# Second products of a feed-forward block, run as two 64-row halves on the TensorE array

## The chip, the cores and the metric

One NeuronCore of a Trainium2 chip runs the whole kernel. The metric is the device time of one execution in microseconds, from launch to the last store. All inputs and the output lie in the chip's memory as fp32.

## The reference, cut to what matters

An input of 2048 positions by 576 channels is normalised over the channels. Two branches read the result, and their sum is added to the input: a state-space convolution along the positions (computed in the kernel as a transform, a product with a kernel spectrum and a transform back), and a feed-forward block of width 4608.

```python
x = A_u
xn = _layernorm(x, axis=-1)
return x + _A_ref(xn, A_A_re, ..., A_Dskip) + _B_ref(xn, B_w1, B_w2)

def _B_ref(x, w1, w2):
    h = jnp.einsum("bsd,df->bsf", x, w1)     # 576 -> 4608, the first product
    h = _silu(h)
    out = jnp.einsum("bsf,fd->bsd", h, w2)   # 4608 -> 576, the second product
    return out
```

## The kernel before, in words

The positions are worked in two halves of 1024, each of two blocks of 512, and the width of 4608 in nine chunks (`NCH`) of four tiles (`FT`) of 128. For every (half, chunk, block) the function `up` computes the first products of the four tiles, and `down` the second products of the block's four groups of 128 positions.

Both products are done in fp32r, a one-pass form of fp32 with a shortened mantissa. To keep precision each operand is split into a high part and a low part, and three products are added: high by high, high by low and low by high. So a first product (`ph`, L331 to L333) is 14 matmuls that move 512 columns each into one PSUM bank. A second product (`po`, L357) covers half of the 576 output channels: 12 matmuls (four tiles of the width, three part products each) that move 288 columns and contract over 128 rows, all adding up in one bank. VectorE then adds that bank to the running sum `acc[j]` in SBUF (L361). There are 288 such sums, so 3,456 second-product matmuls and 288 adds.

The eight PSUM banks are shared by three pools: `ps1` with two banks (the first products), `ps2` with three (the second products, and now and then another tile), and `pss` with three (transposes and everything of the convolution branch).

Beside the feed-forward block runs the convolution branch, as a generator `side()` that is woven into it step by step. Between about 165 and 640 us it builds the convolution kernel: VectorE and ScalarE make tables (`th`, `S`, `C`), TensorE contracts them (`kp`, L696, on columns 32 wide) and transforms the result (`z`, L711). Those `z` matmuls already work on 64-row halves of the array: the two halves of `kt` go to the two halves of the array by `tile_position=(64 * h, 0)`, in turns, each into a bank of its own. From about 640 us on it multiplies the spectra (`pk`, `pu2`, `pb`, L826). In the tail it adds the convolution's result to the running sums (`py`, L847, tiles of 64 rows by 32 columns).

The order of instructions on each engine is not the order of the source. A scheduler decides it at build time: it runs its own model of the engines, picks among the instructions that are ready, and takes the adds of `down` ahead of other VectorE work (`tc.high_priority()`). A tile is given a bank when one is free in that model. Once built, each engine runs its list in order and waits at semaphores.

Of the kernel before, what the change touches and what calls it, by code (L numbers as in the profile page):

```python
# [11 lines left out]
F32 = mybir.dt.float32  # L12
# [7 lines left out]
P = 128  # L20
# [6 lines left out]
HD = D // 2  # L27
# [16 lines left out]
def kernel(  # L44
# [21 lines left out]
    nc = tc.nc  # L66
    FT = 4
# [40 lines left out]
    ps1 = ctx.enter_context(tc.tile_pool(name="ps1", bufs=2, space=PSUM))  # L108
    ps2 = ctx.enter_context(tc.tile_pool(name="ps2", bufs=3, space=PSUM))
    pss = ctx.enter_context(tc.tile_pool(name="pss", bufs=3, space=PSUM))  # L110

    acc = {}
# [27 lines left out]
    pins = {}  # L140
# [27 lines left out]
    def load_x(j, pool, tag, engines):  # L168

        t = pool.tile([P, 2, D], F32, tag=tag, name=f"{tag}{j}")  # L170
        for i in range(2 if j == 0 else 1):
            for ps, v, eng in quarters(xv, engines):
                if j:
                    eng.dma_start(t[ps], v[:, j:j + 2])
                else:
                    eng.dma_start(t[ps, i], v[:, i])
        pairs[j] = t
        return t[:, 0, :], t[:, 1, :]
# [78 lines left out]
    def ffn():  # L257
        w2v = w2.rearrange("(t p) d -> p t d", p=P)
        blocks = [(half, c, b) for half in range(2) for c in range(NCH) for b in range(2)]
        W1, W2, G = {}, {}, {}  # L260
# [83 lines left out]
        def down(blk, jj):  # L344
            half, c, b = blk
            j = 8 * half + 4 * b + jj
            js = slice(jj * P, (jj + 1) * P)
            if half == 1 and c == NCH - 1:
                if jj % 2 == 0:
                    add_conv(j, (acc[j], acc[j + 1]))  # L350
            for h in range(2):
                hs = slice(h * HD, (h + 1) * HD)
                po = ps2.tile([P, 512], F32, tag="ps2", name="po")
                n = 0
                for t in range(FT):
                    for g, w in ((0, 0), (0, 1), (1, 0)):
                        pins["pe"] = nc.tensor.matmul(po[:, :HD], G[blk, t][g][:, js], W2[half, c, t][w][:, hs],  # L357
                                                      start=n == 0, stop=n == 3 * FT - 1).ins
                        n += 1
                with tc.high_priority():  # L360
                    nc.vector.tensor_add(acc[j][:, hs], po[:, :HD], acc[j][:, hs])  # L361
            if half == 0 and c == NCH - 1:
                rows = slice(j * P, (j + 1) * P)
                nc.sync.dma_start(dr0[rows, :], acc[j])
                if j % 2:
                    acc[7 + j], acc[8 + j] = load_x(7 + j, accp, "acc", (nc.sync,))
# [42 lines left out]
        for i, blk in enumerate(blocks):  # L409
            half, c, b = blk  # L410
# [23 lines left out]
            for step in ("u0", "d0", "d1", "d2", "d3", "u1", "u2", "u3"):  # L434
                k = int(step[1])
                if step[0] == "d":
                    down(blk, k)
                    yield 3.0
                elif later:
                    up(blocks[i + 1], k)  # L440
                    yield 3.0
                for f, t in after.get((b, step), ()) if more else ():
                    f(*new, t)
                if half == 0 and c == NCH - 1:
                    for kt in {"d3": (0, 1), "u1": (2, 3), "u2": (4,)}.get(step, ()):
                        split_xt(b, kt)
# [391 lines left out]
    def add_conv(j, dsts):  # L838

        py = [pool.tile([P, 512], F32, tag=t, name="py") for pool, t in ((pss, "pss"),) * 3 + ((ps2, "ps2"),)]  # L840
        first = pins["pe"]
        for n in range(16):
            i, q1, q2, h = 1 - n // 8, n // 4 % 2, n // 2 % 2, 1 - n % 2
            o = 64 * q1 + 32 * q2
            rows = slice(64 * h, 64 * h + 64)
            with tc.high_priority() if n else nullcontext(), behind(first):
                mm = nc.tensor.matmul(py[2 * i + h][o:o + 32, :HD], s4[rows], yss[j + i][rows, 2 * q2 + q1],  # L847
                                      start=True, stop=True, tile_position=(64 * h, o), skip_group_check=True)
            if n == 0:
                first = mm.ins  # L850
        for i in range(2):
            del yss[j + i]
            for h in range(2):
                hs = slice(h * HD, (h + 1) * HD)
                nc.vector.tensor_add(dsts[i][:, hs], py[2 * i + h][:, :HD], dsts[i][:, hs])
        for _ in range(2):
            conv_load()
# [165 lines left out]
```

## Time and profile before

| | |
|---|---|
| median of the runs before | 1111.05 us (1110.82 to 1111.27, two runs) |
| span of the profiled execution | 1108.2 us |
| profiled execution's own time | one of these two runs; some 2.6 to 3.1 us lie outside its span |
| TensorE matmul busy | 1102.2 us, 99% |
| VectorE busy | 916.6 us, 83% |
| ScalarE busy | 706.9 us, 64% |
| GpSimd busy | 72.1 us, 7% |
| chain that ended last | TensorE 98%: second products (L357) 42%, first products (L331 to L333) 41% |
| moved by DMA | 148.56 MB, 134 GB/s on the mean |

The profile shows one execution. PE is TensorE's matmuls, PEld its weight loads, DVE is VectorE, ACT ScalarE, POOL GpSimd and SP the queue that issues most transfers. Matmuls overlap in the array's pipeline, so the duration of one is longer than the distance to the next; what a matmul costs is that distance. "128*128" beside a matmul is the part of the array it uses, rows by columns; "x16" is a count. A row of the timeline has the start, the length, the engine and the instruction.

### The profile page before, as it was taken

What the parts mean: (1) busy time and instruction counts of PE and PEld (TensorE: products, weight loads), DVE (VectorE), ACT (ScalarE), POOL (GpSimd) and SP (SyncE); (2) the same over time, 40 slices, a digit from 0 to 9 for tenths busy, and PEclk for the clock granted to TensorE, in tenths of its full rate; (3) what the DMA queues carried; (4) which work ended last, traced back from release to release, by engine and by line L of the source; (5) the groups of instructions that cost most, each with busy time, mean ns of one, the idle gap of its engine ahead of it and who ended that gap; (6) DMA issues with size and microseconds to landing.
All of it is one profiled execution on the core that took longest, in us unless ns stands there. A gap on an engine that the chain in (4) does not pass through costs nothing.

```text
span 1108.2 us, 22917 instructions
## 1 busy us (share of the span) xinstructions
PE 1102.2 (99%) x9167; PEld 997.5 (90%) x9167; DVE 916.6 (83%) x1543; ACT 706.9 (64%) x1222; POOL 72.1 (7%) x129
## 2 busy tenths in 40 slices
PE   9999999999999999999999999999999999999998
PEld 7989998899998899899999989999999999999887
DVE  7799899999999999999999737787778778784433
ACT  4564466676677676677867536877777878774210
POOL 1100000000000000011000000000000000000111
PEclk9999999999999999999999999999999999999999
DMA  9745512525252525264744173554544455434983
GB/s 270 190 123 160 152 50 61 120 73 131 77 121 83 116 72 118 77 174 154 206 122 103 45 179 109 162 167 123 156 145 152 138 149 170 129 107 127 241 224 87
DMA packets 175755, 148.56 MB, mean 134 GB/s; under 512 B 111088, under 2 KB 142592, under 8 KB 175520
## 3 DMA queue, kind: packets, MB, share of 16 engines
q1 hardware_dynamic: 165328, 112.63, 38.7%
q0 software_dynamic: 9568, 33.62, 9.6%
q8 instruction: 72, 1.18, 0.5%
q10 hardware_dynamic: 752, 0.85, 0.3%
q14 instruction: 35, 0.29, 0.1%
HBM read 102.53 MB, written 44.61 MB: 133 GB/s over the span
## 4 chain that ended last, share of the span: by engine, by line
PE 98%; DMA 1%; DVE 1%; SPq 0%; issue 0%; DVEq 0%
PE po L357 42%; PE ph L331 35%; PE kp L696 3%; PE ph L332 3%; PE ph L333 3%; PE pu L826 2%; PE pb L826 2%; PE pk L826 2%; PE z L711 2%; PE pu L161 1%; PE py L847 1%; DMA acc<-in_A_u_dram 1%; PE pu L162 1%; PE pt L124 0%; DVE w1l L295 0%; PE ptk L490 0%
## 5 line engine op out<-in xcount | busy, mean ns | idle before, releaser
L357 PE MATMUL po<-w2l,gh 128*128 128x288 f32 x1152 | 338.5, 295 | 0.0
L357 PE MATMUL po<-w2h,gl 128*128 128x288 f32 x1152 | 336.4, 295 | 0.0
L357 PE MATMUL po<-w2h,gh 128*128 128x288 f32 x1152 | 336.1, 295 | 0.0
L357 PEld LDWEIGHTS po<-w2h,gh 128*128 128x128 f32 x1152 | 215.2, 188 | 7.7 <-issue 2.8
L357 PEld LDWEIGHTS po<-w2l,gh 128*128 128x128 f32 x1152 | 215.9, 188 | 5.1 <-issue 0.5
L357 PEld LDWEIGHTS po<-w2h,gl 128*128 128x128 f32 x1152 | 215.4, 188 | 0.9
L339 ACT ACTIVATE gf<-ph 128x512 f32<-128x512 f32 (+1 forms) x148 | 86.4, 584 | 143.8 <-PE ph L333 134.8
L331 PE MATMUL ph<-xh,w1l 128*128 128x512 f32 (+1 forms) x592 | 161.3, 385 | 0.0
L331 PE MATMUL ph<-xh,w1h 128*128 128x512 f32 (+1 forms) x592 | 161.3, 387 | 0.0
L331 PE MATMUL ph<-xl,w1h 128*128 128x512 f32 (+1 forms) x592 | 161.1, 385 | 0.0
L361 DVE TENSOR_TENSOR acc<-po,acc 128x288 f32<-128x288 f32 x288 | 126.2, 451 | 37.0 <-PE po L357 35.6
L342 DVE TENSOR_TENSOR gl<-gf,gh 128x512 fp32r<-128x512 f32 (+1 forms) x148 | 99.0, 672 | 64.6 <-ACT gh L340 63.8
L331 PEld LDWEIGHTS ph<-xh,w1l 128*128 128x128 f32 x592 | 108.0, 188 | 20.0
L331 PEld LDWEIGHTS ph<-xl,w1h 128*128 128x128 f32 x592 | 107.9, 188 | 19.8
L331 PEld LDWEIGHTS ph<-xh,w1h 128*128 128x128 f32 x592 | 104.5, 188 | 16.7 <-ACT x L133 0.5
L340 ACT CAST gh<-gf 128x512 fp32r<-128x512 f32 (+1 forms) x148 | 89.5, 608 | 9.5 <-PE po L357 6.6
L653 ACT ACTIVATE c<-th,magic 128x1040 f32<-128x1040 f32 x36 | 42.1, 1168 | 37.9 <-DVE C L676 28.0
L655 ACT ACTIVATE c<-th 128x1040 f32<-128x1040 f32 x36 | 38.7, 1075 | 33.6 <-DVE th L654 33.6
L314 ACT CAST w2h<-w2r 128x576 fp32r<-128x576 f32 x72 | 47.0, 671 | 17.7 <-PE po L357 14.9
L295 DVE TENSOR_TENSOR w1l<-w1r,w1h 128x640 fp32r<-128x640 f32 x72 | 56.9, 817 | 0.2
L332 PE MATMUL ph<-x,w1h 128*128 128x512 f32 (+1 forms) x148 | 57.0, 386 | 0.0
L333 PE MATMUL ph<-x,w1l 128*128 128x512 f32 (+1 forms) x148 | 56.9, 385 | 0.0
(185 smaller groups left out, 1828.8 us busy)
## 6 DMA issues: line engine op xcount, KB each, us to landing
w2r<-in_B_w_dram SPq DMA_DIRECT2D x72, 288.0 KB, 3.8
w1r<-in_B_w_dram SPq DMA_DIRECT2D x35, 512.0 KB, 3.8
d1u<-u POOLq DMA_DIRECT2D x32, 288.0 KB, 2.5
d1k<-stage SPq DMA_DIRECT2D x18, 512.0 KB, 6.8
ur<-d1u SPq DMA_DIRECT2D x32, 288.0 KB, 3.7
kr<-d1k SPq DMA_DIRECT2D x32, 288.0 KB, 2.9
d<-yo POOLq DMA_DIRECT2D x32, 288.0 KB, 4.0
ys<-d SPq DMA_DIRECT2D x32, 288.0 KB, 11.8
```

What stands on the lines that cost most here:

```text
L295: pins["w1l"] = nc.vector.tensor_sub(l1, src, h1).ins
L314: pins["w2h"] = nc.scalar.copy(h2, r2).ins
L331: nc.tensor.matmul(ph, w[:, kt, :], v[:, kt, a:e], start=n + kt == 0, stop=False)
L332: nc.tensor.matmul(ph, h1[:, 4, :], x4[:, a:e], start=False, stop=False)
L333: pins["pe"] = nc.tensor.matmul(ph, l1[:, 4, :], x4[:, a:e], start=False, stop=True).ins
L339: nc.scalar.activation(gf, ph, AF.Silu)
L340: pins["gh"] = nc.scalar.copy(gh, gf).ins
L342: pins["gl"] = nc.vector.tensor_sub(gl, gf, gh).ins
L357: pins["pe"] = nc.tensor.matmul(po[:, :HD], G[blk, t][g][:, js], W2[half, c, t][w][:, hs], start=n == 0, stop=n == 3 * FT - 1).ins
L361: nc.vector.tensor_add(acc[j][:, hs], po[:, :HD], acc[j][:, hs])
L653: nc.scalar.activation(c65, th, AF.Identity, bias=magic)
L826: nc.tensor.matmul(dst, st, mv[:, hs], start=n == 0, stop=n == 3 * len(terms) - 1)
```

## The change

Each matmul of a second product becomes two, over rows 0 to 63 and 64 to 127 of the same operands, at array positions (0, 0) and (64, 0). Each half of the contraction adds up in a bank of its own, so a sum of 12 matmuls in one bank becomes 24 in two banks. The banks come from `ps2`, except that the second bank of every fourth sum comes from `ps1`. VectorE adds both banks to the running sum, one after the other, 576 adds in place of 288.

```diff
             for h in range(2):
                 hs = slice(h * HD, (h + 1) * HD)
-                po = ps2.tile([P, 512], F32, tag="ps2", name="po")
+                po = [pool.tile([P, 512], F32, tag=t, name="po")
+                      for pool, t in ((ps2, "ps2"), (ps1, "ps1") if h and jj % 2 else (ps2, "ps2"))]
                 n = 0
                 for t in range(FT):
                     for g, w in ((0, 0), (0, 1), (1, 0)):
-                        pins["pe"] = nc.tensor.matmul(po[:, :HD], G[blk, t][g][:, js], W2[half, c, t][w][:, hs],
-                                                      start=n == 0, stop=n == 3 * FT - 1).ins
+                        for r in range(2):
+                            rows = slice(64 * r, 64 * r + 64)
+                            pins["pe"] = nc.tensor.matmul(po[r][:, :HD], G[blk, t][g][rows, js],
+                                                          W2[half, c, t][w][rows, hs], start=n == 0,
+                                                          stop=n == 3 * FT - 1, tile_position=(64 * r, 0)).ins
                         n += 1
                 with tc.high_priority():
-                    nc.vector.tensor_add(acc[j][:, hs], po[:, :HD], acc[j][:, hs])
+                    for r in range(2):
+                        nc.vector.tensor_add(acc[j][:, hs], po[r][:, :HD], acc[j][:, hs])
```

## The prediction

> **What bounds the kernel now.** I read the page first: its busy shares, the chain that ended last and the costliest groups.
>
> ```profile
> span 1108.2 us, 22917 instructions
> ...
> PE 1102.2 (99%) x9167; PEld 997.5 (90%) x9167; DVE 916.6 (83%) x1543; ACT 706.9 (64%) x1222; POOL 72.1 (7%) x129
> ...
> PEclk9999999999999999999999999999999999999999
> ...
> PE 98%; DMA 1%; DVE 1%; SPq 0%; issue 0%; DVEq 0%
> ...
> L357 PE MATMUL po<-w2l,gh 128*128 128x288 f32 x1152 | 338.5, 295 | 0.0
> L357 PE MATMUL po<-w2h,gl 128*128 128x288 f32 x1152 | 336.4, 295 | 0.0
> L357 PE MATMUL po<-w2h,gh 128*128 128x288 f32 x1152 | 336.1, 295 | 0.0
> ```
>
> TensorE is the chain: 98% of the span, at full granted clock, never idle before a second product. The mean of 295 ns is the latency of one matmul, since they overlap; what one costs is the pace of a long run. The chain in order of time gives that:
>
> ```profile
> 625.59 6.36 PE po L357 x48
> 1061.51 6.55 PE po L357 x48
> ```
>
> 6.36 / 48 and 6.55 / 48 are 0.1325 and 0.1365 us. I take 0.133 us per second product, so 3,456 of them hold the array for 459.6 us, which agrees with the 42% the page gives L357 (465 us). Then I asked what TensorE waits for, and how full VectorE is in each stage (columns: stretch, length, then busy time of PE, PEld, DVE, ACT, POOL, granted clock, DMA share, GB/s).
>
> ```profile
> PE pz L879 <- DVE zero L874: 1.3, 1, 1.3
> PE pt L124 <- DVE xn L202: 0.4, 2, 0.2
> ...
> 165.00:640.00 475.00, 475.00 (x5083) 428.69 (x5082) 454.00 (x681) 327.98 (x495) 21.52 (x39) 1.00 0.40 108
> 640.00:915.00 275.00, 275.00 (x1728) 254.53 (x1727) 205.68 (x373) 199.80 (x413) 19.77 (x36) 1.00 0.51 150
> ```
>
> TensorE waits 1.7 us in all. VectorE is second: in the long stage it works 454 of 475 us, without ever holding TensorE up. So whatever TensorE is given or spared shows in the span nearly one for one.
>
> **The change part by part.** Each second product becomes two matmuls, over contraction rows 0 to 63 and 64 to 127. They still move 288 columns each. The kernel already has this shape of work: the z matmuls (L711) are 64-row halves of the array that take turns. Their rows price everything, in stretches of the timeline around 501 us (start, length, engine).
>
> ```profile
> 500.61 0.29 PE L357 MATMUL po<-w2l,gh 128*128 128x288 f32 x1
> 500.83 0.38 PE L711 MATMUL z<-f,kt 64*128 64x128 f32 x2
> 500.83 0.97 PEld L711 LDWEIGHTS z<-f,kt 64*128 64x128 f32 x16 [0.16 <-ACT gf L339]
> 500.94 0.41 PEld L711 LDWEIGHTS z<-f,kt 64*128 64x128 f32 x5
> 500.83 1.16 PE L711 MATMUL z<-f,kt 64*128 64x128 f32 x16
> 501.92 0.40 PE L161 MATMUL pu<-sp,s 128*128 128x288 f32 x1
> 502.16 0.29 PE L162 MATMUL pu<-sp,s 128*128 128x288 f32 x1
> 36.14 0.60 PE L124 MATMUL pt<-ident,xn 128*128 128x128 f32 x4
> ...
> L711 PEld LDWEIGHTS z<-f,kt x288: 182/188/189, 174.5 to 642.9; 64*128 64x128 f32 x144
> L711 PE MATMUL z<-f,kt x288: 272/272/374, 174.5 to 643.0; 64*128 64x128 f32 x144
> ```
>
> Four things follow. (1) Two halves do run side by side: the first two z matmuls span 0.38 us together, where one alone lasts at most 0.374, so the second starts under 0.01 us after the first. (2) A half is no cheaper than a whole: 16 z loads span 0.97 us with 0.188 each, so a pair comes every (0.97 - 0.188) / 7 = 0.112 us; four whole transposes (L124) of the same 128 columns come every (0.60 - 0.27) / 3 = 0.11 us. (3) The next load of a half is hidden behind its running matmul: loads go on from 500.94 while the first pair runs. (4) Changing between whole array and halves empties the array: from the last po at 500.61 to the second pu at 502.16 are 1.55 us, holding one po (0.133), 8 z pairs (0.892) and one pu (0.133), in sum 1.158. The other 0.39 us is the two changes, 0.195 us each, part of it the unhidden first load (0.40 against 0.29 for the pu).
>
> By (1) and (2) the best the change can reach for a pair is 0.133 us, what the whole matmul cost. It spares TensorE nothing; the question is what it adds.
>
> *The order.* The source issues the halves in turns, but a scheduler decides TensorE's order, and each half needs its own free bank. In the built program of the changed kernel the turns are often lost:
>
> ```
> L360 po_2824<-w2h_1873,gh_2196 [waits DVE] ... 12 matmuls of po_2824
> L161, L162 pu x4, L331 ph x4
> L360 po_2825<-w2h_1873,gh_2196 [waits DVE] ... 12 matmuls of po_2825
> ```
>
> po_2824 is the lower half, po_2825 the upper half of one sum. TensorE starts its matmuls in order, so twelve of one half in a row use half the array at a time, 0.133 us each. Of 6,912 half matmuls 4,255 follow one of the same half, 2,370 one of the other half, 287 something else. In 106 of the 288 sums the first half is through before the second begins. I walked the order with one rule (a matmul starts when its half is free and the matmul ahead has started): 1,353 start beside a partner, 5,559 take a slot of their own. 5,559 x 0.133 = 739 us against 459.6: **+280 us**. The pace is bounded by its nearest rows: 0.1365 above, and below by the 512-column products, 12 in 2.75 us, or 0.229 each (0.447 ns a column, 0.129 for 288):
>
> ```profile
> 1003.17 2.75 PE ph L331 x12
> ```
>
> *Array changes.* The scheduler weaves second products between first products (L331) and the spectral ones, all on the whole array. Changes of array shape in TensorE's order go from 88 to 561, that is 473 more x 0.195 = **+92 us**. Bounds: 0, if the emptying belongs to z's plain fp32 data and not to the shape, and 0.195 again for doubt above. Against 0: the transposes at 36.14 are plain fp32 on the whole array too, come between po matmuls, and pass at their ordinary pace.
>
> *VectorE.* 288 more adds of one 128x288 bank into the running sum:
>
> ```profile
> L361 DVE TENSOR_TENSOR acc<-po,acc 128x288 f32<-128x288 f32 x288 | 126.2, 451 | 37.0 <-PE po L357 35.6
> ...
> 165.00:640.00 475.00, 55.98 (x129) 1.00 0.40 108
> ```
>
> The second row is the long stage with this line alone. 288 x 0.451 = 130 us, 1,047 us in all. Over a span of some 1,480 us that is 71%, so it hides behind TensorE. In the long stage 129 of the adds fall, 454 + 58 = 512 us, where TensorE's 475 grows by a third or so. What isn't hidden is the wait for banks: a sum holds two banks of five shared with ph, and matmuls of the second product that wait for VectorE go from 301 to 572. Behind such a wait stands all of TensorE, also the first products, then the SiLU and casts on ScalarE. Bounds: 0, as now; and one add for each of the 288 sums, 130 us. I take **+40 us**, nearer to 0, because the order already fills most bank waits by running one half alone (priced above), and VectorE gets freer. At the very end one more add is exposed, **+0.4 us**.
>
> DMA queues: no transfer is added. Loads and stores keep their order within small swaps, and SP, POOL and ACT get more time per transfer as TensorE slows; the cover is TensorE's own work. Without it, nothing is late that isn't late now.
>
> *Sum.* 1108.2 + 280 + 92 + 40 + 0.4 = 1520.6 for the span; 2.9 more lie around it (1111.05 median less 1108.2). **1523 us**, against 1111.05.
>
> **The rivals.**
>
> - *No overlap.* Halves in fp32r on 64 rows aren't shown by any row. If none overlapped, 1,353 more slots of 0.133 are +180: 1703 us. Against it: the z rows. Chance 0.08.
> - *Order doesn't matter.* If each half of the array drained its own queue, the second products would stay at 460 us: 1523 - 280 = 1243. Against: in every row matmuls start in order. Chance 0.05.
> - *Free change of shape.* 1523 - 92 = 1431. For it: only fp32 matmuls are tiled now. Chance 0.06.
> - *Loads show.* If a load couldn't run behind a matmul of its own half, 5,559 slots grow by the unhidden load, 0.40 - 0.29 = 0.11 us: +611, about 2095 with the bank waits gone. Against: the z loads from 500.94, and a pair in 0.112. Chance 0.04. The Trainium skill (TensorE: Matmul & The Clock Gate, Part 3, The mechanism) states just this: a load overlaps running matmuls only where its row group differs. This trace disagrees, for whole-array and 64-row loads alike.
> - *VectorE holds the banks.* Each sum waits for one more add: 1523 + 90 = 1613. For it: 454 of 475 us. Against: TensorE slows more than VectorE is loaded. Chance 0.12.
> - *Not slower.* If a 64-row matmul in fp32r streamed in half the time, 0.0665, slots would fill 370 us, 90 less than now, and the shape changes would eat just that: 1108.2 - 90 + 92 + 3.3 = 1114. It decides from a half's price of 0.07 downward. Against: 0.112 for 64 rows beside 0.11 for 128. Chance 0.02.
>
> **How the numbers follow.** My forecast has 0.63. Its own range, from the pace (0.129 to 0.1365: -22 to +19) and the bank waits (-40 to +40), is some 1460 to 1585. The 8-in-10 range takes in the free change below and VectorE's wait above: 1430 to 1615; left out are 0.08 + 0.05 + 0.04 + 0.02. A measurement can tell about 2% here (22 us). Faster by that 0.01 and the same 0.01 share the last rival; slower has 0.98.
>
> **What would show it.** Right: TensorE still over 95% busy and on the chain; long runs of one half at 0.133 us a matmul; pairs starting within 0.01 us; some 0.3 us between the last whole-array matmul and the second half matmul after a change; VectorE near 1,040 us busy but about 70%. Wrong: solo runs at 0.24 us (loads show), pairs 0.133 us apart (no overlap), no gap at a change, or TensorE idle behind VectorE for over 100 us.

## The result and the profile after

The changed kernel takes 1591.8 us at the median (1591.08 to 1592.53, two runs) against 1111.05 before: a ratio of 1.433, 95% interval 1.429 to 1.437. The forecast was 1523 with a range of 1430 to 1615. The page of the changed kernel, the lines that answer to those of before:

```profile
span 1589.3 us, 30247 instructions
...
PE 1528.9 (96%) x12623; PEld 1319.2 (83%) x12623; DVE 1047.3 (66%) x1831; ACT 717.1 (45%) x1222; POOL 72.3 (5%) x129
...
PEclk9978998999898768998988789999999999979999
...
PE 73%; DVE 16%; ACT 4%; DMA 4%; issue 2%; SPq 1%; POOL 0%; DVEq 0%; ACTq 0%; POOLq 0%
...
L360 PE MATMUL po<-w2h,gh 64*128 64x288 f32 x2304 | 600.2, 335 | 46.5 <-DVE acc L366 32.9
...
L366 DVE TENSOR_TENSOR acc<-po,acc 128x288 f32<-128x288 f32 x576 | 254.9, 452 | 185.7 <-PE po L360 176.9
```

TensorE is still 96% busy, and yet the chain leaves it for 27% of the span. VectorE has its 576 adds, 1,047 us busy, and falls to 66%. New is the clock row: digits of 6, 7 and 8 where before all were 9.

What TensorE waits for, and the granted clock by stage (columns of the second: stretch, length, busy time of PE, PEld, DVE, ACT, POOL, granted clock, DMA share, GB/s):

```profile
PE po L360 <- DVE acc L366: 32.9, 23, 4.3
PE po L360 <- ACT gh L340: 13.5, 1, 13.5
```

```profile
250.00:900.00 650.00, 622.64 (x5768) 543.41 (x5767) 461.04 (x726) 303.40 (x450) 19.97 (x36) 0.88 0.29 75
...
1500.00:1589.00 89.00, 84.37 (x850) 72.39 (x848) 38.93 (x86) 10.35 (x17) 9.70 (x21) 0.99 0.37 100
```

The waits are small, 33 us for the adds. The lower clock sits where the table building and the second products run side by side. Now TensorE's timeline (start, length, engine, instruction), a run with partners, a run of one half, and a change of array shape:

```profile
441.03 0.30 PE L360 MATMUL po<-w2l,gh 64*128 64x288 f32 x2
441.16 0.30 PE L360 MATMUL po<-w2h,gl 64*128 64x288 f32 x2
441.30 0.29 PE L360 MATMUL po<-w2h,gh 64*128 64x288 f32 x1
441.43 0.29 PE L360 MATMUL po<-w2l,gh 64*128 64x288 f32 x1
...
447.49 0.29 PE L162 MATMUL pu<-sp,s 128*128 128x288 f32 x1
447.71 0.40 PE L360 MATMUL po<-w2h,gh 64*128 64x288 f32 x2
447.95 0.30 PE L360 MATMUL po<-w2l,gh 64*128 64x288 f32 x2
```

A row with x2 is a pair: two halves within 0.30 us, where one takes 0.29. The next row comes 0.13 us later, whether it holds two halves (441.03 to 441.16) or one (441.30 to 441.43). So a half without a partner costs what a pair costs. From the last whole-array matmul to the second pair are 0.46 us (447.49 to 447.95), where two slots would be 0.27: the change costs 0.19.

TensorE does not start its halves strictly in the order of its list, though the description of the kernel and the prediction take that for granted:

```profile
456.30 0.29 PE L360 MATMUL po<-w2l,gh 64*128 64x288 f32 x1
456.31 0.40 PE L360 MATMUL po<-w2h,gh 64*128 64x288 f32 x1
456.43 0.29 PE L360 MATMUL po<-w2h,gl 64*128 64x288 f32 x1
```

One half takes a slot of 0.133 us, so starts 0.01 us apart (456.30 and 456.31) are on different halves of the array. The built list has the lower half's matmuls of 456.30 and 456.43 and two more lower ones ahead of the upper half's matmul that starts at 456.31. Followed by their operands and banks through list and trace, 986 of the 6,912 half matmuls start ahead of one to three earlier ones of the other half, and only 12 ahead of more. So a half that is free runs ahead by up to three places of the list, and 1,628 of the 3,456 possible pairs start under 60 ns apart, many of them out of step.

And a stretch of the same kernel some 70 us later, the window from 522.6 to 543 us first:

```profile
522.60:543.00 20.40, 20.40 (x86) 18.60 (x87) 7.57 (x15) 2.64 (x5) 0.54 (x1) 0.50 0.34 77
```

```profile
522.59 0.60 PE L360 MATMUL po<-w2h,gh 64*128 64x288 f32 x1 [0.61 <-DVE acc L366]
523.00 0.44 PE L360 MATMUL po<-w2l,gh 64*128 64x288 f32 x1
523.24 0.44 PE L360 MATMUL po<-w2h,gl 64*128 64x288 f32 x1
523.48 0.44 PE L360 MATMUL po<-w2h,gh 64*128 64x288 f32 x1
```

At a clock of 0.50 a half takes a slot of 0.24 us (523.00, 523.24, 523.48). There are 19 such stretches, 249.6 us in all, of which only the last (3.8 us) lies behind the work.

To see what each costs I put every interval between the starts of two consecutive matmuls into one class. *Slots* is the matmul's own pace (0.133 us for 288 columns); *shape* is what stands above it at a change of array shape and one interval behind it, and the few ns between partners; *waits* are gaps over 0.1 us; *half clock* is what stands above the pace while the clock is 0.50. The borders are not sharp, since a wait at a change or at half clock can fall on either side: another rule for them moves 10 to 30 us between the last three classes. The row of the changed kernel is rounded. Microseconds from the first matmul to the last:

| kernel | slots | shape | waits | half clock | sum |
|---|---|---|---|---|---|
| before | 1080.1 | 15.9 | 6.4 | 0.0 | 1102.3 |
| after | 1322 | 123 | 65 | 74 | 1583.5 |
| difference | +242 | +107 | +58 | +74 | +481 |

### The profile page after: what moved, and what is told of

The parts are those of the page before. It is cut to its first block, busy times and chain, and to the rows that moved or that the text cites. A ratio compares the mean times of both kernels' runs of the same rounds, so it can differ in the third digit from the quotient of the medians.

```text
span 1589.3 us, 30247 instructions
## 1 busy us (share of the span) xinstructions
PE 1528.9 (96%) x12623; PEld 1319.2 (83%) x12623; DVE 1047.3 (66%) x1831; ACT 717.1 (45%) x1222; POOL 72.3 (5%) x129
## 4 chain that ended last, share of the span: by engine, by line
PE 73%; DVE 16%; ACT 4%; DMA 4%; issue 2%; SPq 1%; POOL 0%; DVEq 0%; ACTq 0%; POOLq 0%
PE po L360 36%; PE ph L331 23%; DVE acc L366 2%; PE pb L831 2%; PE pu L831 2%; PE pk L831 2%; PE ph L332 2%; PE ph L333 2%; DVE C L669 2%; PE kp L701 1%; DMA ys<-d 1%; DVE S L680 1%; DVE th L659 1%; DVE C L680 1%; DVE th L642 1%
## 5 line engine op out<-in xcount | busy, mean ns | idle before, releaser
L360 PE MATMUL po<-w2h,gh 64*128 64x288 f32 x2304 | 600.2, 335 | 46.5 <-DVE acc L366 32.9
L360 PE MATMUL po<-w2l,gh 64*128 64x288 f32 x2304 | 561.9, 313 | 0.0
L360 PE MATMUL po<-w2h,gl 64*128 64x288 f32 x2304 | 556.8, 314 | 0.7 <-DVE gl L342 0.7
L360 PEld LDWEIGHTS po<-w2h,gh 64*128 64x128 f32 x2304 | 364.9, 200 | 105.7 <-DVE acc L366 43.0
L366 DVE TENSOR_TENSOR acc<-po,acc 128x288 f32<-128x288 f32 x576 | 254.9, 452 | 185.7 <-PE po L360 176.9
L360 PEld LDWEIGHTS po<-w2l,gh 64*128 64x128 f32 x2304 | 371.1, 202 | 6.8 <-issue 6.1
L360 PEld LDWEIGHTS po<-w2h,gl 64*128 64x128 f32 x2304 | 367.9, 201 | 10.3 <-issue 8.4
L331 PE MATMUL ph<-xh,w1h 128*128 128x512 f32 (+1 forms) x592 | 178.2, 423 | 3.1 <-DVE acc L366 2.0
L314 ACT CAST w2h<-w2r 128x576 fp32r<-128x576 f32 x72 | 46.7, 671 | 127.8 <-PE po L360 109.3
L316 DVE TENSOR_TENSOR w2l<-w2r,w2h 128x576 fp32r<-128x576 f32 x72 | 53.8, 750 | 22.4 <-ACT w2h L314 22.2
L680 DVE TENSOR_TENSOR S<-th,C 128x1024 f32<-128x1024 f32 x36 | 44.0, 1221 | 21.7 <-ACT th L661 21.4
```

Source lines behind the costliest of these rows:

```text
L314: pins["w2h"] = nc.scalar.copy(h2, r2).ins
L316: pins["w2l"] = nc.vector.tensor_sub(l2, r2, h2).ins
L331: nc.tensor.matmul(ph, w[:, kt, :], v[:, kt, a:e], start=n + kt == 0, stop=False)
L360: pins["pe"] = nc.tensor.matmul(po[r][:, :HD], G[blk, t][g][rows, js], W2[half, c, t][w][rows, hs], start=n == 0, stop=n == 3 * FT - 1, ti ...
L366: nc.vector.tensor_add(acc[j][:, hs], po[r][:, :HD], acc[j][:, hs])
L680: nc.vector.tensor_mul(ov3, t[:, :, 0:64].rearrange("n d (x y) -> n d x y", y=32), mv3)
```

## Experiments

The theory to test is that of the prediction: halves that run without a partner, changes of shape, and waits for banks. The rivals: the loss is the waits for VectorE, or the half clock, and the halves without a partner only fill time that would be lost anyway.

### e1: the prices by themselves

Runs of the same matmuls in a kernel by themselves (288 columns, fp32r): whole ones (`wh`), pairs (`pr`), halves alone (`so`), four whole and four pairs in turns (`sw`, `pr`), and groups of twelve with a wait for two adds between, as whole ones (`wg`) and as halves (`sg`).

> A kernel of its own with second-product-like matmuls only (288 columns, fp32r, data from the input; the reference is not computed): 120 whole, then 120 pairs of 64-row halves in turns, then 240 of one half alone, then 20 times 4 whole and 4 pairs, then 16 groups of 12 whole and 16 groups of 12 of one half, each group with a wait for two VectorE reads of its bank. My theory: 0.133 us for a whole, for a pair and for a single half alike; 0.195 us for each change between whole array and halves; the clock stays full in the long run of one half (about half of the array's rows in use), stays full in the groups of whole matmuls with waits (array in use about 0.58 of the time), and falls to half only in the groups of one half with waits (0.58 of the time, half the rows, about 0.29). Rival, the clock follows waits alone: it falls in both kinds of groups or in neither. Rival, halves do not overlap: 0.266 us a pair.

```profile
34.95 16.32 PE pr L50 x229
51.26 32.23 PE so L50 x240
83.50 8.26 PE wh L41 x60
...
98.81 0.73 PE sw L41 x4
100.27 0.73 PE sw L41 x4
```

These are pieces of the chain in order of time: start, length, what. 240 halves alone take 32.23 us, 0.134 each; 120 pairs 16.32, 0.136 each (the chain follows 229 of their 240 matmuls); 60 whole ones 8.26, 0.138 each with the last one's latency in it. Four whole and four pairs come round every 1.46 us (98.81 to 100.27), 8 x 0.133 and two changes of 0.195. Then the two kinds of groups, windows first, then a group of each in the timeline:

```profile
120.00:185.00 65.00, 48.33 (x333) 44.26 (x333) 17.77 (x39) 0.00 (x0) 0.00 (x0) 1.00 0.00 1
185.50:250.00 64.50, 49.90 (x188) 44.77 (x187) 13.74 (x30) 0.00 (x0) 0.00 (x0) 0.50 0.00 1
```

```profile
157.60 1.86 PE L41 MATMUL wg<-mv,wt 128*128 128x288 f32 x12 [1.04 <-DVE acc L56]
...
201.62 3.25 PE L50 MATMUL sg<-mv,wt 64*128 64x288 f32 x12 [1.04 <-DVE acc L56]
```

In the run of pairs the two halves drift out of step, up to 56 ns and back, without losing pace. The same waits of 1.04 us leave whole-array groups at full clock and put groups of halves at half clock, where twelve take 3.25 us in place of 1.86. The runs of halves without waits kept full clock. So the prices of the prediction stand, and a fifth one appears, which it lacked.

### e2: strict turns

Each half is put right behind the other half of its pair in TensorE's list; banks and adds stay.

```diff
-                            pins["pe"] = nc.tensor.matmul(po[r][:, :HD], ...
+                            with behind(prev):
+                                prev = nc.tensor.matmul(po[r][:, :HD], ...
```

> The changed kernel with the two halves of a sum forced to take strict turns. In its order 3,528 slots of 0.133 us remain for second products (469 us, 10 more than before) and 483 changes of array shape (395 more than before, 77 us). My theory: 1108 + 10 + 77 + about 50 of bank waits as in the changed kernel + 3 = about 1248 us, granted clock 1.0, since both halves of the array work. Rival, the clock follows TensorE's waits alone: clock 0.92 to 0.95 and 1300 us or more. Rival, the pairs themselves are slow: about 1590 us as the changed kernel.

Measured 1585.04 us (1582.9 to 1586.69), ratio 1.4273 (1.4249 to 1.4297): the time of the changed kernel, 337 above what I expected. The edit did what it should: 3,349 of 3,456 pairs run side by side (1,628 in the changed kernel, taken as starts under 60 ns apart). By the classes, slots fall from 1322 to 1100.0 us. But waits go from 65 to 263.6, and the half clock's cost from 74 to 105.5. Waits, then one of them on TensorE and on VectorE:

```profile
PE po L362 <- DVE acc L369: 204.7, 140, 7.6
```

```profile
682.75 0.29 PE L362 MATMUL po<-w2h,gh 64*128 64x288 f32 x1
687.27 0.60 PE L362 MATMUL po<-w2h,gh 64*128 64x288 f32 x1 [4.23 <-DVE acc L369]
```

```profile
682.13 1.22 DVE L683 TENSOR_TENSOR S<-th,C 128x1024 f32<-128x1024 f32 x1
683.27 0.68 DVE L684 SCALAR_TENSOR_TENSOR S<-th,C 128x512 f32<-128x512 f32 x1
683.87 1.22 DVE L683 TENSOR_TENSOR C<-c,C 128x1024 f32<-128x1024 f32 x1
685.01 0.69 DVE L684 SCALAR_TENSOR_TENSOR C<-c,C 128x512 f32<-128x512 f32 x1
685.61 1.24 DVE L645 TENSOR_TENSOR th<-vt,fT 128x1040 f32<-128x1040 f32 x1
686.76 0.45 DVE L369 TENSOR_TENSOR acc<-po,acc 128x288 f32<-128x288 f32 x1
```

TensorE stands for 4.23 us because the add that frees its bank stands behind five pieces of table work on VectorE, which runs its list in order. So the step "no halves alone, no +280" is not disproved, but what the turns spare came back as waits. The numbers of both rivals came true too (clock 0.93, some 1590 us), but not their reasons: in e1 a pair costs 0.136 us, and whole-array groups keep the clock through waits. Two causes were left: too few places for sums, or lists made at build time that suit the halves badly.

### e3: no turns at all

All twelve matmuls of the lower half, then all of the upper half.

```diff
-                for t in range(FT):
-                    for g, w in ((0, 0), (0, 1), (1, 0)):
-                        for r in range(2):
+                for r in range(2):
+                    for t in range(FT):
+                        for g, w in ((0, 0), (0, 1), (1, 0)):
```

> The changed kernel with all 12 matmuls of the lower half of a sum forced ahead of the 12 of the upper half. 6,411 slots of 0.133 us (853 us, 393 more than before), 496 changes (80 us more). My theory: 1108 + 393 + 80 + 35 of waits + 3 = 1619 us at full clock, and half-clock stretches longer than the changed kernel's 250 us, so 1680 to 1850 us. Rival, the clock follows TensorE's waits alone: fewer half-clock stretches than in the changed kernel, since its order has fewer waits for VectorE (523 against 579), 1620 to 1700 us.

Measured 1689.57 us, one run, inside both ranges, so the time alone doesn't choose between them. What chooses is the time at half clock: 22 stretches, 375.5 us in all against 249.6, though TensorE waits no longer for the adds (28.9 us against 32.9). The theory had longer stretches, the rival fewer. Slots rise to some 1387 us. 1,114 pairs are left, where a start in the order of the list would leave some 500, since halves run ahead; that is 514 fewer than in the changed kernel, 65 us for 514 slots, 0.13 each. The half clock costs some 118 us:

```profile
PEclk9886997988988578898878789999999999779789
```

### e4: two banks without halves

Whole-array matmuls, alternating between the two banks of a sum; both banks are added.

```diff
-                        for r in range(2):
-                            ... matmul(po[r][:, :HD], G[blk, t][g][rows, js], ...
+                        ... matmul(po[n % 2][:, :HD], G[blk, t][g][:, js], ...
```

> The changed kernel's two banks and two adds for each sum, but with whole-array matmuls, even ones into one bank and odd ones into the other: no halves, 90 changes of array shape (88 before). My theory: VectorE's 288 more adds and the banks cost only TensorE's waits, 10 to 60 us: 1120 to 1170 us, clock 1.0. Rival, the adds and the bank demand are the main cost: over 1250 us.

Measured 1213.24 us (1211.05 to 1214.35), ratio 1.0919 (1.0903 to 1.0935), above the 1170 that I had as the upper end. So the second banks and the second adds by themselves cost 102 us, though TensorE's work is the same: waits 87.3 us in place of 6.4, half clock 16.8.

```profile
PE po L358 <- DVE acc L364: 45.3, 39, 5.1
```

### e5, e6 and e7: the banks of a sum as one tile

The three single banks of `ps2` become two tiles of two banks, and every sum takes one tile; `pss` gives up a bank for it. e5 runs whole-array matmuls in these tiles, e6 the halves of the changed kernel with nothing else edited, and e7 the same halves in strict turns, with the list of every engine taken over from e5 (each whole matmul replaced by its pair).

```diff
-    ps2 = ctx.enter_context(tc.tile_pool(name="ps2", bufs=3, space=PSUM))
-    pss = ctx.enter_context(tc.tile_pool(name="pss", bufs=3, space=PSUM))
+    ps2 = ctx.enter_context(tc.tile_pool(name="ps2", bufs=2, space=PSUM))
+    pss = ctx.enter_context(tc.tile_pool(name="pss", bufs=2, space=PSUM))
...
-                po = [pool.tile([P, 512], F32, tag=t, name="po")
-                      for pool, t in ((ps2, "ps2"), (ps1, "ps1") if h and jj % 2 else (ps2, "ps2"))]
+                both = ps2.tile([P, 2, 512], F32, tag="ps2", name="po")
+                po = [both[:, r, :] for r in range(2)]
```

> The second products run as whole-array matmuls, alternating between the two banks of one double tile, and VectorE adds both banks; no halves. Two double tiles (four banks) stand where the changed kernel shares five single banks among the sums. All theories: this is the price of second banks and second adds without any half. Nearest row: the run with two single banks at 1213. Expected 1190 to 1260, TensorE over 90% busy, granted clock over 0.97, about 136 array-shape changes. If banks alone are what the changed kernel lacks, already this run is over 1350.

> The same banks as the run before it, with the second products as halves, and every engine's list as the build's scheduler makes it; the order has almost no solo slots and 740 shape changes. Theory (lists): the lists are made for a TensorE on which each half fills a slot, so that adds stand behind VectorE work that is due too early and TensorE waits for banks: 1500 to 1620, with over 150 us of TensorE waits for VectorE, as in the run with strict turns. Rival (banks): the same time, but then the run with fitted lists is no faster. Rival (half clock alone): granted clock under 0.93 explains over 200 us of it and the waits are under 80 us.

> The same halves, banks and adds, in strict turns, but each engine's list is the one of the kernel with whole-array products in double tiles (each whole matmul replaced by its pair); 593 shape changes against 136 there. Theory (lists): pairs cost what whole matmuls cost, and the changes add 457 x 0.195 = 89 us, so the time is that of the whole-array run plus 80 to 130 us: 1270 to 1380, TensorE waits for VectorE under 80 us, clock over 0.96. Rival (banks): within 50 us of the run with the scheduler's own lists, 1480 or more. Rival (half clock comes from halves as such): clock under 0.93 and over 1450.

e5 measured 1278.16 us (1277.65 to 1284.83), ratio 1.1524 (1.1495 to 1.1553); e6 1350.48, one run; e7 1348.53 (1347.23 to 1349.1), ratio 1.2146 (1.2125 to 1.2166). The page's lines of e6, the waits of e6 and then of e7:

```profile
span 1348.7 us, 30128 instructions
...
PE 1258.1 (93%) x12623; PEld 1029.1 (76%) x12623; DVE 1043.9 (77%) x1831; ACT 707.1 (52%) x1222; POOL 72.1 (5%) x129
...
PEclk9999999999999999999999999999999999998999
```

```profile
PE po L361 <- DVE acc L367: 32.3, 27, 4.6
```

```profile
PE po L393 <- DVE acc L404: 37.6, 32, 3.0
```

e5 lies 18 us above the end of its range, and 65 above e4: for whole matmuls the double tiles, with a bank less for `pss`, are worse than the single banks. For e6 every theory missed: I expected 1500 to 1620, and the scheduler's own lists are as good as the fitted ones of e7 (1350 against 1349). So the lists are not the cause where the banks come in pairs, though e7 itself lies in the range that the theory gave it (1270 to 1380). What did it is the banks: the same halves, adds and contraction as the changed kernel, and 241 us less. The classes show how:

| kernel | pairs | slots | shape | waits | half clock |
|---|---|---|---|---|---|
| after | 1,628 | 1322 | 123 | 65 | 74 |
| e2, turns, single banks | 3,349 | 1100.0 | 106.3 | 263.6 | 105.5 |
| e4, whole, single banks | | 1083.8 | 16.8 | 87.3 | 16.8 |
| e5, whole, double tiles | | 1083.0 | 17.0 | 109.4 | 60.5 |
| e6, halves, double tiles | 3,402 | 1095.9 | 146.0 | 96.6 | 4.1 |
| e7, e6 with e5's lists | 3,453 | 1070.5 | 121.9 | 89.8 | 57.2 |

From after to e6 slots fall by 226 us, the half clock's cost by 70 (58 us at half clock in place of 250), shape rises by 23 and waits by 32 (681 changes in the list in place of 567): that sums to -241. This is the test that e2 was meant to be. My reading is that with three single banks the next sum gets one bank of its two early and the other late; the scheduler fills the time with halves alone (after), or, where turns are forced, TensorE stands still (e2). I counted TensorE's work, at 0.133 us a slot, between the matmul that last wrote a bank and the one that takes it again: in e2's built list it is under 1 us for 114 of 576 banks, in e4's for 6, in e6's for none. Whether another list for VectorE alone would have helped e2 with its three banks was not tried and stays open. Nor do the runs separate the pairing of the banks from their number: e6 gives the sums four banks of their own, where the changed kernel has three and, for every fourth sum, one of `ps1`. Four single banks were not run.

e7 against e5 is the price of halves with everything else alike: +70 us. Of that shape is +105 for 447 more changes, 0.19 each once 18 us between partners are taken off; slots and waits give some back. The pairs themselves bring nothing: 3,453 of them cost as many slots as the whole matmuls.

### e8 and e9: adds and places apart

e8 is the kernel before with two adds of the same bank, so that every second product counts twice; e9 is the kernel before with its sums in two double tiles of which one bank is used, and one add.

```diff
-                    nc.vector.tensor_add(acc[j][:, hs], po[:, :HD], acc[j][:, hs])
+                    for _ in range(2):
+                        nc.vector.tensor_add(acc[j][:, hs], po[:, :HD], acc[j][:, hs])
```

> Second products as in the kernel before (whole array, one bank for each sum), but VectorE adds the same bank twice, so the running sum takes each second product twice. This is the price of the 288 extra adds (0.45 us each, 130 us of VectorE) by themselves. In the build's order a bank is taken again 3.5 us or more after its last matmul for 95 in 100 sums, as before. Theory (banks): TensorE waits for VectorE stay under 25 us, 1112 to 1140. Rival (adds): VectorE's extra work delays all its results, 1170 to 1230, since two adds and two banks together cost 102 us (three single banks) and 167 us (double tiles).

> Second products as in the kernel before (whole array, one bank, one add for each sum), but the sums rotate over two double tiles, of which only the first bank is used, in place of three single banks. This is the price of two places in place of three, with no extra add. In the build's order half of the sums take a place under 4.3 us after its last matmul, 46 of 288 under 2 us. Theory (banks): TensorE waits of 50 to 110 us and stretches at half clock behind them, 1170 to 1270. Rival (adds): 1112 to 1140.

e8 measured 1165.91 us (1159.83 to 1167.85), ratio 1.0492 (1.0463 to 1.0521), between the two expectations; e9 1206.47 (1202.32 to 1207.33), ratio 1.0854 (1.0834 to 1.0873), as the theory had it. So both cost something by themselves. In e8 it is waits (46.7 us by the classes, 40 more than before), spread over what TensorE needs from VectorE and ScalarE; the adds alone hold it for 16 us:

```profile
PE po L357 <- DVE acc L362: 16.2, 13, 3.5
PE ph L331 <- ACT gf L339: 6.7, 5, 3.0
```

In e9 waits are +44 us and half clock +51. The half clock comes late, here the clock row and a window of the convolution stage:

```profile
PEclk9999999999999999999999999999999999867799
```

```profile
1060.00:1160.00 100.00, 70.72 (x371) 57.19 (x379) 50.99 (x96) 48.13 (x108) 10.38 (x20) 0.75 0.63 164
```

There `pss` has two banks in place of three, and of TensorE's waits from 1040 to 1135 us 20.6 are for ScalarE to empty a bank of `pss` (`kb`, L756), which the kernel before never waits for. So part of what e9 pays, and by the same late stretches e5 and e7, is the bank that `pss` gave up, and not the second product's places.

No kernel here beats the one before: a pair costs what a whole matmul costs, so the best of them only approaches it from above.

## Why the prediction was right, and where not

The direction, the size and most of the mechanism came out. The forecast was 69 us short, and the classes tell by which term. That it is no more is in part luck: one term was too large, three were too small.

- *Pairs run side by side, at the price of a whole matmul*: right. Partners in step start 3 to 5 ns apart (timeline), and pairs come every 0.13 us (timeline, e1), in step or not.
- *Halves alone*, +280 us: the right term, 38 us too large, +242. The order was walked to 1,353 pairs, on the rule that a matmul starts only when the one ahead has started; the trace breaks that rule by up to three places and has 1,628. The 1,828 slots more than before at 0.133 us are 243 us. e6 takes most of them away and gains 226 us on this term.
- *Changes of shape*, +92: right, +107, of which some 19 are the few ns between partners. (107 - 19) / 471 more changes is 0.19 us each against 0.195, and e1 has 0.195 for fp32r itself, which rules out the lower bound of 0. The Trainium skill (TensorEngine Tiling (Array Packing), Key Properties) says that changing the tiling mode drains TensorE; it gives no time for it, and the traces have 0.19 to 0.20 us.
- *VectorE and banks*, +40: too small, +58. It was taken nearer to 0, "because the order already fills most bank waits by running one half alone". That is so in the changed kernel (33 us behind the adds). But second banks with second adds cost 102 us with no half at all (e4), and second adds alone 56 (e8), so I read the cover as bought with the slots.
- *Full clock*: wrong, and the step that failed. The sum had no term for it, since the kernel before holds 1.00 in every window. Half clock costs some +74 us. Term by term the miss is -38 (halves alone) + 15 (shape) + 18 (waits) + 74 (clock) = 69.
- *VectorE at 1,040 us and some 70%*: 1,047.3 and 66%. TensorE over 95% busy: 96%, but on the chain only for 73%, which I had taken for sure.

Of the rivals, no overlap, free changes and loads that show are all refuted by the timeline above and e1. That order doesn't matter is refuted as it was put (1243 us), but its ground holds in part, since a half runs up to three places ahead. Halves alone at 0.133 us with their loads hidden are also against the rule of the Trainium skill cited in the prediction. "VectorE holds the banks" gave 1613 and came nearer to the time than the forecast, but for another reason than its own: TensorE's waits are 58 us more, not 130.

## What to carry to other kernels

Splitting a contraction into row halves of the array saves nothing when each half still moves the same columns; it can only lose partners, and each loss is a full slot. Give the two accumulation banks of such a sum as one tile, two tiles in all (1350 us against 1592); whether four single banks would do as well was not run, and for whole matmuls three single banks were better (1213 against 1278). The scheduler's filler of halves alone looks like busy time (96% here). When a busy engine gets slower, split its intervals into pace, shape changes, gaps and clock before naming a cause, and distrust an experiment that removes one of them until you have seen that no other took its place.

## What the runs showed of the hardware

Half-array matmuls with short waits between drop the granted clock to one half; whole-array ones with the same waits do not (e1: 1.04 us after each group of twelve, 0.50 against 1.00), and half-array ones without waits do not either (32 us at full clock). Two halves of the array need not start in the order of the list: one runs ahead of up to three matmuls of the other. To read the drops of the kernels I weighed the streaming time of a window of 3.4 us by the share of the array's rows in use (an estimate from starts and paces; 1 is the whole array without a gap). In the changed kernel each of the 18 drops ahead of the last matmul follows a window of 0.42 or less, and of 372 other windows at full clock one lies under that (0.41). Whole-array kernels drop too when they wait long enough: in e4, e5 and e9 each drop follows a window of 0.39 or less. In e2, e3, e5, e7, e8 and e9 one to four windows each of 0.25 to 0.39 were not followed by one. The way back is higher: in all runs the clock rose only behind a window of 0.69 or more. A half that runs alone is at 0.5 by itself, so waits of some fifth of the window start a drop, and halves alone do not end it. That the clock goes by such a weight is a reading of these windows; e1 tests it directly, e3 agrees. The Trainium skill (TensorE: Matmul & The Clock Gate, Part 1, HAM oscillation — how this bites in real kernels) states the rule as no idle gaps above some 3.4 us; here gaps of 1.04 us were enough between groups of halves, and not between whole-array groups (e1). The length of the low stretches, multiples of 3.4 us in the changed kernel (6.8, 10.2, 13.7, 20.5 us), agrees with the window of that page.
